# One attention block and a gated FFN on one core: batch 1's queries turned by DMA, batch 0 turned by products, gates begun in halves, and a new written order

## The chip, the core and the metric

The kernel runs on one core of one Trainium2 chip. The core has TensorE (PE, matrix products, with its weight loads shown as PEld), VectorE (DVE), ScalarE (ACT), GpSimd (POOL) and SyncE (SP), and 16 DMA engines. Each engine works through its own instructions in order; semaphores join them. PE writes into PSUM, which has eight banks of 128 x 512 f32. The metric is device time in microseconds, lower is better.

## The reference

Four batches of 768 tokens, eight heads of width 64. Each token attends to the 8 first keys (global) and to the 96 keys up to itself (local), with a bias that falls with distance; the result goes through a gated FFN.

```python
B, H, S, D = q.shape                                  # 4, 8, 768, 64
scores = scale * np.matmul(q, k.transpose(0, 1, 3, 2))
rel = pos[:, None] - pos[None, :]
is_global = pos[None, :] < 8
is_local = (rel >= 0) & (rel < 96)
dist = np.where(is_global & ~is_local, 96.0, np.abs(rel))
scores = scores - slopes[:, None, None] * dist        # then -1e9 where neither
a = softmax(scores); attn = np.matmul(a, v)
x = attn.transpose(0, 2, 1, 3).reshape(B * S, H * D)  # 3072 x 512
g = x @ w_gate                                        # 512 x 1536
out = (g * sigmoid(g) * (x @ w_val)) @ w_out          # 1536 x 512
```

## The kernel before

**Tiling.** The 3072 tokens are eight tiles of 384, two (halves) per batch. For a batch the eight heads form four pairs `hp`. Keys lie in 14 chunks of 64 rows: 8 global and 56 local ones; a chunk serves a window of 152 queries. Chunks are packed into units of two to four; batch 0 has other units (0 and 1 for its first half, 2 to 4 for its second), so that half 0 can go ahead.

**Attention steps.** Each step is a word in the string `ORDER`, followed by its numbers, and `@n` names a PSUM bank.

- `Lh`, `L4`, `Lr` load queries (i = 1) and keys (i = 0) of batch 0 by halves, of batch 1 four heads at a time, of batches 2 and 3 by single heads in 256-byte rows (L249, L287, L292). `Lv`, `Lt`, `LG` load V (L255, L261, L266), `Lw` a quarter-height piece of a gate or value weight (L299), `Lo` a third of `wo` (L307). All of these are issued by POOL and turn f32 into f16 on the way.
- `VG` loads the 8 global V rows of batch 0 (L271) and `Gc` copies them into the 14 chunks (L277); later batches do this by `G`, a DMA of SP (L283).
- `T` and `U` turn queries and keys of batches 0 and 1 on PE with an identity matrix, 8 and 16 turns a step (L358, L399); `k`, `q`, `kw`, `qw` copy the turned data out of PSUM (L367, L372, L390, L412). For batches 2 and 3 `D` turns by a DMA of SP (L420), and `K` spreads the keys into chunks (L427 to L430).
- `c` makes scores (L448), `x` exponentials on ACT (L457), `m` multiplies by a mask on DVE (L478). `w.b.h.0` sums the rows (L505), `w.b.h.1` and `.2` weigh V (L511), `i` and `r` invert and spread the sums (L521 to L529), `p` scales into `xT` on DVE (L540), one of two sides a step: blocks 0 and 2, or 1 and 3.

**FFN steps.** `g.t.f` and `v.t.f` make 128 gate or value columns of tile t, four products of 384 columns each (L553); `t` is a tanh on ACT (L559), `s` and `h` make the hidden block on DVE (L563, L570). `o.t.i.part` adds a quarter of the output of 128 tokens (L588; L585 for the last 128 tokens, in two halves of 256 columns), and `e` evicts it on ACT and stores it through SP (L602, L603; L597 to L600 for the last). `fill` are products of ones whose result nobody reads (L338).

**What sets the order.** The string alone: every engine gets its instructions in the order in which the steps stand. POOL's loads take turns on eight semaphores, so a load is not issued before the eighth one ahead of it has landed. The pool `st` has 7 buffers for loaded queries and keys, `qT` 6, `kN` (keys turned by DMA) 3, `at` 14. SP carries, in one queue, the first small loads, `G`, `D` and the output stores; a `D` that waits holds the stores behind it, and the other way round.

Of the kernel before, what the change touches and what calls it, by code (L numbers as in the profile page):

```python
# [16 lines left out]
CH = 64  # L17
# [41 lines left out]
m.0.0.4.V m.0.1.2.V t.0.4 s.0.7 g.0.0@2 t.0.5 Lw.1.1.1 m.0.0.2.V Lw.1.1.0 m.0.1.3.V m.0.1.4.V  # L59
v.0.4@4 Lv.0.0.7.13 t.0.0 s.0.5 s.0.4 m.0.0.3.V h.0.4 Lt.0.0 t.0.3 v.0.7@5 Lw.1.0.1 Lw.1.0.0 v.0.6@3  # L60
v.0.5@6 h.0.7 g.0.2@1 w.0.1.0@4 Lv.0.5.7.13 Lv.0.2.7.13 Lv.0.7.7.13 t.0.6 s.0.6 s.0.0 Lv.0.4.7.13
Lv.0.3.7.13 h.0.5 v.0.2@5 v.0.3@0 v.0.1@2 s.0.3 i.0.1 h.0.6 t.0.2 r.0.1 s.0.2 Lv.0.1.7.13 L4.1.1
Gc.1.1.A w.0.1.2@6 p.0.1.1 w.0.1.1@3 LG.1.0 g.0.1@1 v.0.0@6 p.0.1.0 h.0.2 Lw.0.2.1 g.1.1@7 L4.0.0
L4.0.1 v.1.6@3 Lw.1.2.0 h.0.3 t.0.1 s.0.1 g.1.4@5 h.0.0 v.1.3@0 g.1.3@1 t.1.1 t.1.4 s.1.1 s.1.4
v.1.4@4 t.1.3 g.1.6@7 s.1.3 Lw.0.2.0 g.1.0@5 Lw.1.2.1 h.0.1 t.1.0 s.1.0 v.1.0@6 h.1.0 h.1.4 Lo.1
t.1.6 v.1.1@1 Lo.0 Lv.1.4.0.13 h.1.1 U.3.0@2 kw.3.A Lo.2 U.1.1@5 U.2.1@6 U.1.0@4 U.0.0@1 s.1.6
qw.2.A h.1.3 g.1.2@2 g.0.9@7 U.2.0@6 kw.1.A Lr.2.1.3 g.1.7@0 g.0.8@4 t.1.2 s.1.2 kw.0.V h.1.6
v.1.2@2 qw.1.A t.0.9 Lr.2.1.2 Lr.3.1.1 Lv.2.3.0.13 t.1.7 s.0.9 v.0.8@3 v.1.7@5 s.1.7 Lv.1.2.0.13
Lv.1.1.0.13 h.1.2 Lt.1.1 LG.3.1 LG.1.1 v.0.9@1 g.0.10@7 Lv.1.6.0.13 t.0.8 v.0.10@0 s.0.8 h.1.7
kw.2.A Lr.3.0.6 t.0.10 c.1.0.0@4 h.0.8 c.1.0.2@2 U.3.1@6 s.0.10 v.0.11@7 x.1.0.2 m.1.0.2.V x.1.0.0  # L70
o.0.0.0@2 g.0.11@3 t.0.11 qw.3.V h.0.9 o.0.1.0@4 o.0.1.1 c.1.1.1@5 h.0.10 s.0.11 c.1.0.1@0 x.1.0.1
Lr.2.0.0 o.0.1.2 h.0.11 o.0.1.3 e.0.1 o.0.0.1 o.0.0.2 o.0.0.3 e.0.0 x.1.1.1 o.0.2.0@3 G.1.0 g.1.11@0
g.1.5@1 t.1.11 t.1.5 Lv.3.7.0.13 Lr.2.0.2 Lt.1.0 G.1.1 s.1.5 Lt.2.0 Lv.2.5.0.13 o.0.2.1 Lv.1.3.0.13
Lr.2.1.7 Lv.1.0.0.13 c.1.1.2@4 c.1.1.0@6 o.0.2.2 o.0.2.3 s.1.11 x.1.1.0 v.1.11@1 m.1.1.1.V g.1.10@0
Lv.3.6.0.13 g.1.8@6 h.1.11 m.1.0.0.V x.1.1.2 v.1.5@7 e.0.2 v.1.10@2 v.1.9@1 v.1.8@4 m.1.1.0.V
m.1.1.2.V t.1.10 Lv.1.5.0.13 t.1.8 s.1.8 h.1.5 c.1.0.3@5 m.1.0.1.V h.1.8 w.1.0.0@3 x.1.0.3 o.1.0.0@7
# [24 lines left out]
Lt.3.1 Lr.3.0.3 s.4.1 g.4.7@3 t.4.8 g.4.5@5 t.4.5 m.2.1.4.V s.4.8 g.4.4@6 v.4.8@1 g.4.11@7 h.4.1
# [31 lines left out]
def kernel(  # L133
# [525 lines left out]
```

## Time and profile before

| | |
|---|---|
| median of the runs shown | 245.4 us (245.36, 245.4, 252.1) |
| the profiled execution, in all | 247.71 us |
| its span, first to last instruction | 245.6 us |
| PE busy | 234.9 us, 96% of the span |
| DVE, ACT, POOL busy | 162.3, 105.4, 87.0 us |
| gate and value products (L553), wg and wv | 72.6 and 72.2 us, 384 each |
| output products (L588) | 64.6 us, 276 |
| turns on PE, batch 0 (L358), batch 1 (L399) | 6.1 and 3.7 us, 128 each |
| loads by POOL's queue | 14.20 MB written, 64656 packets |
| mean granted PE clock | 0.979 of full |

Busy times are those of single instructions merged, so an engine is busy where anything of its runs. Matmuls overlap, so their mean lengths add up to more than their share of time; what one costs in a row of many is read from the chain, where the steps of one engine follow one another. In the groups, the last column is the idle time of the engine just before them, with what ended it. In the slices of the span each digit is the busy share of a fortieth, 6.1 us.

### The profile page before, as it was taken

How to read it: one execution, taken by the hardware profiler on the slowest of the kernel's cores; microseconds unless marked ns; L12 is line 12 of the kernel's file. 1: busy time of each engine (PE TensorE's matmuls, PEld its weight loads, DVE VectorE, ACT ScalarE, POOL GpSimd, SP SyncE). 2: the span in 40 equal slices, each digit the busy share in tenths (PEclk: the TensorE clock that was granted, in tenths of full speed). 3: DMA queues.
4: the chain of work that ended last, by engine and by line, in shares of the span. 5: the costliest groups of instructions: out<-in, count | busy, mean ns of one | idle time of the engine just before them, and what ended most of it. 6: DMA issues, size and time to landing. Idle time of an engine off the chain costs nothing.

```text
span 245.6 us, 7237 instructions
## 1 busy us (share of the span) xinstructions
PE 234.9 (96%) x3112; PEld 137.3 (56%) x3112; DVE 162.3 (66%) x359; ACT 105.4 (43%) x191; POOL 87.0 (35%) x117
## 2 busy tenths in 40 slices
PE   8599999999999999999699999999999999999994
PEld 5376566664554555555355466545555655556643
DVE  5398998785275577837577769834898478505840
ACT  5495733745632533225573253235761142323321
POOL 8698695545999976980000000000000000000000
PEclk9858999999999999999999999999999999999999
DMA  7999999999999999999900374012000300021012
GB/s 103 161 160 161 179 141 178 206 195 91 173 173 144 180 137 160 120 159 200 115 3 0 120 168 42 0 45 88 3 0 15 121 0 3 0 85 43 3 42 86
DMA packets 82095, 24.57 MB, mean 100 GB/s; under 512 B 68896, under 2 KB 79120, under 8 KB 82064
## 3 DMA queue, kind: packets, MB, share of 16 engines
q0 software_dynamic: 64656, 14.20, 65.2%
q1 hardware_dynamic: 17224, 9.77, 18.5%
q8 instruction: 24, 0.39, 0.6%
q10 hardware_dynamic: 184, 0.14, 0.2%
q14 instruction: 7, 0.06, 0.1%
HBM read 28.51 MB, written 6.29 MB: 142 GB/s over the span
## 4 chain that ended last, share of the span: by engine, by line
PE 82%; DMA 9%; DVE 3%; POOL 2%; issue 1%; ACT 1%; ACTq 0%; POOLq 0%
PE PS L553 47%; PE PS L588 25%; PE PS L511 3%; DMA kN<-st 3%; DMA st<-in_q_dram 3%; DMA wv<-in_moe_w_val_dram 3%; PE PS L448 3%; PE PS L505 2%; PE PS L399 1%; PE PS L585 1%; POOL st L249 1%; DVE vS L277 1%; DVE qT L390 1%; ACT th L559 1%; DVE at L478 0%
## 5 line engine op out<-in xcount | busy, mean ns | idle before, releaser
L563 DVE SCALAR_TENSOR_TENSOR sl<-th,PS 128x384 f32<-128x384 f32 x96 | 50.8, 549 | 41.0 <-ACT th L559 40.4
L553 PE MATMUL PS<-xT,wg 128*128 128x384 f16 x384 | 72.6, 326 | 2.2 <-DVE hT L570 2.1
L553 PE MATMUL PS<-xT,wv 128*128 128x384 f16 x384 | 72.2, 326 | 0.1
L559 ACT ACTIVATE th<-PS 128x384 f32<-128x384 f32 x96 | 44.3, 491 | 59.0 <-PE PS L553 50.0
L588 PE MATMUL PS<-wo,hT 128*128 128x512 f16 x276 | 64.6, 379 | 0.0
L570 DVE TENSOR_TENSOR hT<-PS,sl 128x384 f16<-128x384 f32 x96 | 50.9, 552 | 10.4 <-PE PS L553 8.8
L553 PEld LDWEIGHTS <-wg 128*128 128x128 f16 x384 | 36.9, 98 | 28.2 <-issue 2.8
L553 PEld LDWEIGHTS <-wv 128*128 128x128 f16 x384 | 36.7, 98 | 25.6 <-DMA wv<-in_moe_w_val_dram 0.5
L588 PEld LDWEIGHTS <-hT 128*128 128x128 f16 x276 | 26.0, 98 | 28.7
L457 ACT ACTIVATE at<-PS 128x912 f16<-128x912 f32 (+1 forms) x40 | 31.6, 830 | 22.7 <-PE PS L448 22.6
L255 POOL DMA_DIRECT2D vS<-in_v_dram x40 | 33.2, 845 | 8.4 <-DMA wo<-in_moe_w_out_dram 3.0
L602 ACT ACTIVATE osb<-PS 128x512 f32<-128x512 f32 x23 | 13.7, 597 | 41.2 <-PE PS L588 41.2
L478 DVE TENSOR_TENSOR at<-at,masks 128x912 f16<-128x912 f16 (+5 forms) x56 | 22.5, 442 | 1.9 <-ACT at L457 1.9
L540 DVE TENSOR_TENSOR xT<-PS,rb 128x768 f16<-128x768 f32 x16 | 14.6, 952 | 7.2 <-PE PS L511 6.7
L292 POOL DMA_DIRECT2D st<-in_q_dram x16 | 14.4, 915 | 3.1 <-PE PS L553 1.4
L292 POOL DMA_DIRECT2D st<-in_k_dram x16 | 14.2, 912 | 0.5 <-DMA vS<-in_v_dram 0.5
L448 PE MATMUL PS<-qT,kT 64*64 64x152 f16 (+4 forms) x464 | 13.5, 238 | 0.5 <-DVE xT L540 0.4
L448 PEld LDWEIGHTS <-kT 64*64 64x64 f16 x464 | 8.6, 113 | 7.9 <-issue 6.8
L511 PE MATMUL PS<-at,vS 64*32 64x152 f16 (+4 forms) x1024 | 10.5, 218 | 0.4 <-issue 0.4
L511 PEld LDWEIGHTS <-vS 64*32 64x32 f16 x1024 | 9.3, 90 | 2.6 <-issue 2.3
L338 PE MATMUL PS<-ones 128*128 128x256 f16 x44 | 9.1, 387 | 1.2 <-DVE wg L304 1.2
L358 PE MATMUL PS<-ident,st 96*64 96x96 f16 x128 | 6.1, 268 | 3.0 <-DMA st<-in_k_dram 2.6
(50 smaller groups left out, 115.1 us busy)
## 6 DMA issues: line engine op xcount, KB each, us to landing
out_dram<-osb SPq DMA_DIRECT2D x23, 256.0 KB, 3.7
vS<-in_v_dram POOLq DMA_DIRECT2D x24, 91.0 KB, 5.6
wg<-in_moe_w_gate_dram POOLq DMA_DIRECT2D x6, 256.0 KB, 5.7
wv<-in_moe_w_val_dram POOLq DMA_DIRECT2D x6, 256.0 KB, 7.2
wo<-in_moe_w_out_dram POOLq DMA_DIRECT2D x3, 512.0 KB, 14.8
st<-in_q_dram POOLq DMA_DIRECT2D x16, 96.0 KB, 7.2
st<-in_k_dram POOLq DMA_DIRECT2D x16, 96.0 KB, 5.2
st<-in_q_dram POOLq DMA_DIRECT2D x4, 192.0 KB, 7.5
```

Source lines behind the costliest of these rows:

```text
L255: nc.gpsimd.dma_start(out=v_of(b)[CH * c + NG:CH * c + CH, c0:c1, j, :], in_=v[b, h, KC * c0:KC * c1, :].rearrange("(i p) d -> p i d", p=KC))
L292: nc.gpsimd.dma_start(out=stage(b, i, h % 2, True)[:, h // 4, :, h // 2 % 2, :], in_=KQ[i][b, h].rearrange("(t p) d -> p t d", p=128))
L448: nc.tensor.matmul(PS[64 * e:64 * e + 64, bank + hi, col:col + n], lhsT=kT_of(b, hp)[r, CH * c:CH * c + CH], rhs=qTs[b, hp][r, q0:q0 + n], ...
L457: nc.scalar.activation(out=at[:, :, 0:w], in_=PS[:, bank:bank + 2, 0:w], func=AF.Exp, scale=scale)
L478: ENG[e].tensor_mul(a2, a2, m2)
L511: nc.tensor.matmul(PS[r, bank + e, o:o + n], lhsT=V[s, c, j, what - 1::2], rhs=at[s, hi, col:col + n], start=first, stop=last, skip_group_ ...
L540: nc.vector.tensor_mul(x_of(2 * b + half)[:, side::2, :], PS[:, bank:bank + 2, 0:TB], rbs[b, half])
L553: nc.tensor.matmul(PS[:, bank, 0:TB], lhsT=w[:, c, 128 * f:128 * f + 128], rhs=xTs[t][:, c, :], start=(c == 0), stop=(c == NC - 1))
L559: nc.scalar.activation(out=th, in_=PS[:, gv[t, f, 0], 0:TB], func=AF.Tanh, scale=0.5)
L563: nc.vector.scalar_tensor_tensor(out=sl, in0=gv[t, f, "t"], scalar=1.0, in1=PS[:, gv[t, f, 0], 0:TB], op0=AluOp.add, op1=AluOp.mult)
L570: nc.vector.tensor_mul(hTs[t, f // 3][:, f % 3, :], PS[:, gv[t, f, 1], 0:TB], gv[t, f, "s"])
L588: nc.tensor.matmul(PS[:, bank, :], lhsT=lhsT, rhs=wo[:, f, :], start=(f == 0), stop=(f == NFF - 1))
```

## The change

- **Batch 1's queries by DMA.** The two four-head loads of queries become eight loads of single heads; four `tr_dma` steps of SP turn them, in place of four `U` steps and their copies `qw`. Batch 1's keys stay with `L4` and `U`.
- **Global V rows in fp16.** A step `Ga` copies the 8 rows of each side from f32 to f16 once (8 x 256); the four `Gc` copies then read f16. In the order all four stand ahead of batch 0's first keys; before, two stood later.
- **Batch 0 turned by products.** `T` issues an ordinary matmul with the identity as the moving operand, and its result in PSUM is f32 where it was f16.
- **First gates in halves.** The four blocks are added up in the order 0, 2, 1, 3, the order in which the two `p` steps give them. For f = 0 and 1 of the first tile the sum is split: `ga`, `va` add blocks 0 and 2, `gb`, `vb` blocks 1 and 3.
- **Last rows as 384 + 128 columns.** The last 128 tokens make 384 columns first, with their eviction on ACT, then all twelve products of the last 128 columns, evicted on DVE; both stores go through SP.
- **A new order** of all steps. The last `fill` behind the last output goes; 44 fill products stay, now all ahead of the first gate.
- Functions `ld_wide` and `widen_ident` are new, and no step of the order calls them.

The diff, cut; of the order only the part up to the first gates, the output of tile 0 and the end are shown:

```diff
-pre Y.0.1.0 Ld.S Y.0.0.0 Lh.1.0.0.2 Z.1 VG.S.0 Z.2 fill.4@0 fill.4@1 fill.4@2 fill.4@3 VG.A.1 Li.S
-fill.4@4 Lh.0.0.2.4 Z.0 M.0 fill.4@5 M.1 Gc.0.0.V Lh.0.0.0.2 T.1.0.1@6 q.1.0.V T.2.0.0@7 T.1.0.0@0
-Lh.1.1.2.4 M.3 T.0.0.0@1 T.0.0.1@2 Gc.0.1.A T.2.1.1@3 k.2.0.A k.1.0.V Lh.1.0.2.4 LG.2.1 Lh.1.1.0.2
-T.3.1.1@4 q.3.1.A q.0.0.V k.0.0.A T.3.0.1@5 q.3.0.V T.3.0.0@6 T.2.0.1@7 M.2 q.2.0.V T.1.1.1@0
-k.3.0.A T.0.1.1@4 q.2.1.V Lh.0.1.2.4 q.0.1.A c.0.1.1@1 c.0.0.0@5 Gc.1.0.V x.0.1.1 T.2.1.0@7 x.0.0.0
-k.2.1.V Lv.0.1.0.7 Lv.0.5.0.7 q.1.1.V Lh.0.1.0.2 T.3.1.0@3 k.3.1.A c.0.0.1@1 Lw.0.1.0 x.0.0.1
-m.0.1.1.V c.0.1.0@4 m.0.0.0.V x.0.1.0 T.1.1.0@6 T.0.1.0@7 Lv.0.2.0.7 k.0.1.V k.1.1.V c.0.1.2@0
-x.0.1.2 L4.1.0 Lv.0.0.0.7 fill.4@3 fill.4@2 Lv.0.7.0.7 Lv.0.3.0.7 m.0.1.0.V fill.4@5 m.0.0.1.V
-w.0.0.0@7 i.0.0 c.0.0.2@0 Lv.0.4.0.7 x.0.0.2 fill.4@6 c.0.0.3@2 x.0.0.3 Lv.0.6.0.7 Lw.0.1.1
-Lv.0.6.7.13 w.0.0.2@4 r.0.0 Lw.0.0.0 c.0.1.4@0 w.0.0.1@6 p.0.0.1 c.0.0.4@2 x.0.0.4 x.0.1.4 c.0.1.3@4
-p.0.0.0 U.0.1@2 qw.0.A Lw.0.0.1 g.0.7@3 t.0.7 x.0.1.3 g.0.6@0 Lt.0.1 g.0.4@1 g.0.5@6 g.0.3@7
...
+pre VG.S.1 Li.S VG.S.0 Z.1 Z.2 Lh.0.1.2.4 fill.2@3 fill.2@3 fill.2@0 Ld.A fill.2@1 Z.0 Ga.0.A Ga.1.V
+M.1 M.3 fill.2@7 fill.4@2 Lh.1.0.0.2 Lh.0.0.0.2 Gc.0.1.V Lh.1.0.2.4 Lh.0.0.2.4 Lh.1.1.0.2 fill.4@3
+M.0 Gc.1.1.A Gc.1.0.V T.1.0.1@4 Lh.0.1.0.2 fill.2@5 fill.4@2 Lv.0.5.0.7 Y.0.0.0 Gc.0.0.V fill.4@6
+Lv.0.7.0.7 Lv.0.3.0.7 Lv.0.0.0.7 T.2.1.0@0 T.1.0.0@1 q.1.0.A Lh.1.1.2.4 T.0.0.1@7 T.0.0.0@5 k.1.0.V
+k.0.0.A q.0.0.A T.3.0.1@4 T.2.0.1@3 Lv.0.4.0.7 Lw.1.0.0 q.3.0.V Lv.0.6.0.7 Lv.0.2.0.7 T.2.0.0@5
+T.3.0.0@1 k.3.0.A c.0.0.1@6 fill.4@2 T.1.1.1@4 q.2.0.V c.0.0.0@1 fill.4@3 Lv.0.1.0.7 x.0.0.1 k.2.0.V
+M.2 m.0.0.1.V c.0.1.1@5 k.2.1.V fill.4@3 x.0.0.0 q.1.1.V m.0.0.0.V x.0.1.1 T.1.1.0@7 T.3.1.0@3
+k.3.1.A Lw.0.0.1 Lw.0.0.0 Lv.0.7.7.13 c.0.1.0@0 T.0.1.1@2 q.0.1.A T.0.1.0@4 m.0.1.1.V k.1.1.A
+T.3.1.1@5 T.2.1.1@6 fill.2@3 x.0.1.0 Lw.1.0.1 fill.2@2 Lw.0.1.1 Lv.0.0.7.13 k.0.1.V q.2.1.A
+c.0.0.4@3 c.0.0.3@0 m.0.1.0.V x.0.0.4 w.0.0.0@7 x.0.0.3 q.3.1.V Y.0.1.0 c.0.1.3@4 w.0.0.1@2
+m.0.0.4.V i.0.0 r.0.0 Lt.0.1 c.0.1.4@0 Lw.0.1.0 Lv.0.3.7.13 x.0.1.3 w.0.0.2@6 Lv.0.1.7.13 L4.0.1
+m.0.0.3.V p.0.0.0 c.0.0.2@4 x.0.1.4 Lt.0.0 Lv.0.5.7.13 Lv.0.2.7.13 c.0.1.2@2 p.0.0.1 Lv.0.4.7.13
+Lw.1.1.1 ga.0.0@0 x.0.1.2 Lv.0.6.7.13 ga.0.1@1 gb.0.1 va.0.1@7 m.0.1.4.V t.0.1 va.0.0@6 Lw.1.1.0
...
+c.1.1.0@0 o.0.2.0@7 o.0.1.1 h.0.8 h.1.3 c.1.1.1@5 x.1.1.0 D.1.0.1 x.1.1.1 c.1.1.2@0 x.1.1.2 t.1.8
+m.1.1.2.V s.1.8 o.0.1.2 m.1.1.1.V o.0.1.3 e.0.1 o.0.2.1 o.0.2.2 o.0.2.3 o.1.2.0@3 Lv.1.7.0.13
...
+o.7.1.2 o.7.1.3 e.7.1 o.7.2.0@1 o.7.2.1 o.7.2.2 o.7.2.3 e.7.2 o.7.2.4@2 e.7.3

+    def narrow_first_globals(c, e):
+        r = slice(CH * c, CH * c + NG)
+        copy_on(e)(out=first16[r, :], in_=first[r, :])
...
-            in_=first[r, :].unsqueeze(1).broadcast_to([NG, 7, 4 * D]))
+            in_=first16[r, :].unsqueeze(1).broadcast_to([NG, 7, 4 * D]))
...
-                nc.tensor.transpose(
-                    t16[64 * hi:64 * hi + 64, PT * j:PT * j + PT],
-                    stage(0, i, half)[:, head(hp, hi), D * j:D * j + D], ident)
+                nc.tensor.matmul(
+                    PS[64 * hi:64 * hi + 64, bank, PT * j:PT * j + PT],
+                    lhsT=stage(0, i, half)[:, head(hp, hi), D * j:D * j + D], rhs=ident,
+                    start=True, stop=True, skip_group_check=True)
...
+    SIDES = (0, 2, 1, 3)
+    def products(bank, t, f, which, blocks):
...
-        for c in range(c0, c1):
+        for c in blocks:
...
-                rhs=xTs[t][:, c, :], start=(c == 0), stop=(c == NC - 1))
+                rhs=xTs[t][:, c, :], start=(c == SIDES[0]), stop=(c == SIDES[-1]))
...
+    LC = 384
...
+        c = slice(0, DM) if not last_rows(t, i) else slice(LC, DM) if part == 4 else slice(0, LC)
+        for f in range(NFF) if part == 4 else range(3 * part, 3 * part + 3):
...
+        if i == 3:
+            bank = at_bank["o", t, 2, 1]
+            oB = sb2.tile([128, DM - LC], FP32, name="osb", tag="th", bufs=3)
+            nc.vector.tensor_scalar_mul(oB, PS[:, bank, 0:DM - LC], 0.5)
+            nc.sync.dma_start(out=out[r0:r0 + 128, LC:], in_=oB)
+            return
...
+        "ga": lambda bk, t, f: products(bk, t, f, 0, SIDES[:2]),
+        "gb": lambda t, f: products(None, t, f, 0, SIDES[2:]),
```

More of the change, by code (lines that the diff above doesn't have):

```diff
@@ L59 @@
[L59 to L64, printed above, removed]
@@ L215 @@
     wo = sb.tile([128, NFF, DM], FP16, name="wo")
+    ident32 = sb.tile([PT, PT], FP32, name="ident32")
+    wide = {}
     first = sb.tile([128, 4 * D], FP32, name="first")
+    first16 = sb.tile([128, 4 * D], FP16, name="first16")
     KQ = (k, q)
@@ L251, in ld_half, with ld_wide, widen_ident @@
             in_=KQ[i][0, h, TB * half:TB * half + TB, :].rearrange("h (p j) d -> p h (j d)", p=PT))
+    def ld_wide(e, i, p, hi):
+        g = p // 2
+        if (i, g) not in wide:
+            wide[i, g] = sb.tile([PT, 2, JH, 2, D], FP32, name=f"wide{i}{g}")
+        QUE[e].dma_start(
+            out=wide[i, g][:, p % 2, :, hi, :],
+            in_=KQ[i][0, head(p, hi), 0:TB, :].rearrange("(p j) d -> p j d", p=PT))
+    def widen_ident():
+        nc.vector.tensor_copy(out=ident32, in_=ident)
     def ld_v(b, h, c0, c1):
@@ L378, in keys_half @@
         k3 = chunked(0, hp)
-        t3 = turned(at_bank["T", hp, half, 0], JH)
+        t3 = turned(at_bank["T", hp, half, 0], JH, True)
         if half == 0:
@@ L545 @@
     hTs, gv = {}, {}
-    def products(bank, t, f, which, c0, c1):
-        if c0 == 0:
+    SIDES = (0, 2, 1, 3)
+    def products(bank, t, f, which, blocks):
+        if blocks[0] == SIDES[0]:
             gv[t, f, which] = bank
@@ L591, in put_out @@
[L591 to L603 removed]
+        if part in (0, 4):
+            at_bank["o", t, i, part // 4], = bank
```

189 lines of the change are left out of this document (92 added, 97 removed).

## The prediction

> **What bounds the kernel now.** First the shares of the span and the slices of the page, to see which engine is never free, and when:
>
> ```profile
> PE 234.9 (96%) x3112; PEld 137.3 (56%) x3112; DVE 162.3 (66%) x359; ACT 105.4 (43%) x191; POOL 87.0 (35%) x117
> PE   8599999999999999999699999999999999999994
> PEclk9858999999999999999999999999999999999999
> DMA  7999999999999999999900374012000300021012
> PE 82%; DMA 9%; DVE 3%; POOL 2%; issue 1%; ACT 1%; ACTq 0%; POOLq 0%
> ```
>
> TensorE (PE) is busy in every slice but the first three and the last, the DMA engines through the first half. A busy PE is not a useful one, so next come stretches, from the view that gives each engine's busy time by stretch, and two merged lines of PE's timeline:
>
> ```profile
> 12.00:18.00 6.00, 5.84 (x135) 4.56 (x137) 5.28 (x12) 5.46 (x14) 6.00 (x9) 0.50 1.24 157
> 10.20:25.50 15.30, 14.31 (x404) 10.74 (x399) 13.40 (x34) 9.72 (x19) 13.84 (x20) 0.67 1.41 159
> 25.60:60.00 34.40, 34.27 (x506) 20.87 (x506) 28.37 (x63) 18.48 (x33) 20.52 (x29) 1.00 1.37 171
> 111.00:124.00 13.00, 10.85 (x113) 6.07 (x111) 8.38 (x21) 7.10 (x14) 0.00 (x0) 1.00 1.16 147
> 124.00:241.80 117.80, 117.80 (x1414) 67.09 (x1413) 77.47 (x159) 44.56 (x82) 0.00 (x0) 1.00 0.15 43
> ...
> 25.57 4.06 PE L553 MATMUL PS<-xT,wg 128*128 128x384 f16 x24
> 120.34 2.11 PE L553 MATMUL PS<-xT,wg 128*128 128x384 f16 x12 [2.06 <-DVE hT L570]
> ```
>
> Columns: stretch, length, then PE, weight loads, DVE, ACT, POOL busy, granted clock, DMA share, GB/s. Three parts show. Up to 25.57 us, where the first gate product starts, DVE is the busy engine (13.40 of 15.30 us) and the clock is partly halved. From 25.6 to 124 PE loses 0.13 us before 60 and 2.15 between 111 and 124. After 124 it never stops. So the time is the moment of the first gate, plus PE's own work, plus PE's waits, plus a tail after 241.8. A shorter order can save only in these four.
>
> **The change, part by part.** The unit costs of PE's work come from the chain of work that ended last (start, length, what, count):
>
> ```profile
> 33.18 0.57 PE PS L505 x36
> 35.81 1.32 PE PS L511 x134
> 45.13 1.99 PE PS L399 x80
> 54.29 0.52 PE PS L448 x24
> 59.14 3.99 PE PS L588 x18
> 111.41 8.12 DMA kN<-st
> 196.26 15.06 PE PS L553 x92
> ```
>
> *Batch 1's queries by DMA.* Four of eight `tr_whole` calls go, 16 turns each: 64 turns at 1.99/80 = 0.025 us take 1.6 us off PE, in a stretch where PE never idles, so all of it counts: **-1.6**. The evictions of these turns leave ACT and DVE too; neither is on the path there, so I count nothing. What comes instead is transfer work, priced below.
>
> *The key wait.* The 2.06 us of idle PE at 118 to 120 hang on DVE, which stood in `spread_keys` behind a key transpose that SP issued at 111.41 and that took 8.12 us; `tr_dma` for pair 2 of batch 2 stood in SP's queue behind the output rows of tile 2. In the new order SP issues the key transposes of pairs 0, 1 and 2 of batch 2 ahead of those outputs, and only pair 3 has to wait for a buffer. Their last row is POOL's 92nd load of 119 instead of the 95th of 113. The wait goes, **-2.1**; late next is pair 1 (a rival below).
>
> *The first gate.* These rows are DVE's and PE's timeline:
>
> ```profile
> 9.82 0.70 PE L358 MATMUL PS<-ident,st 96*64 96x96 f16 x24 [2.56 <-DMA st<-in_k_dram]
> 14.50 1.99 DVE L277 CAST vS<-first 8x1792 f16<-8x1792 f32 x1
> 16.42 0.66 DVE L367 COPY kT<-PS 128x8 f16<-128x8 f16 x3
> 18.48 2.60 PE L338 MATMUL PS<-ones 128*128 128x256 f16 x12
> 23.69 1.82 DVE L540 TENSOR_TENSOR xT<-PS,rb 128x768 f16<-128x768 f32 x2
> ...
> L390 DVE COPY qT<-PS 128x384 f16<-128x384 f16 x6 | 3.2, 547 | 2.0 <-PE PS L358 2.0
> ...
> L563 DVE SCALAR_TENSOR_TENSOR sl<-th,PS 128x384 f32<-128x384 f32 x96 | 50.8, 549 | 41.0 <-ACT th L559 40.4
> ...
> L478 DVE TENSOR_TENSOR at<-at,masks 128x912 f16<-128x912 f16 x2 | 1.2, 612 | 0.0
> L478 DVE TENSOR_TENSOR at<-at,masks 128x96 f16<-128x96 f16 x3 | 0.6, 194 | 0.0
> ```
>
> The keys that release DVE's run land at 9.8 in both orders (third load in each). From there to the end of `scaled` at 23.69 + 1.82 = 25.51 DVE runs nearly without a gap. The new order takes out of this run two query evictions (2 x 0.55), the 1.99 us copy of the global V rows, one set of half-1 key copies (0.66) and, as the gates begin with blocks 0 and 2, the second `scaled` (0.91): 4.66 us. It puts in a set of key copies that ACT made before (0.66), a query eviction (0.55), and the masks of two more units (0.61 and 2 x 0.19): 2.2 us. That gives 23.0 for the first `scaled`. But ACT gets the moved copies on top of its 9.72 us, in line with the exponentials that the masks wait for. So the ends are 23.0 and 25.5; I take the middle, 24.2. The first two half gates last 4 x 0.164 = 0.65 us and the second `scaled` 0.91, so PE waits 0.26 before the second halves. The gain is 25.57 - 24.2 - 0.26: **-1.1** (from -2.3 to +0.2).
>
> No row shows the fp16 copy of the global rows. All four copies now stand ahead of the first keys, where DVE waits anyway, so even at 1.99 us each they cost nothing; if the rows landed late, at most one copy (2.0) would fall on the run. *Turning by products* writes f32 where the transpose wrote f16, with the same operands. DVE's copy of 384 out of PSUM took 547 ns from f16 against 549 in the gates (L563) from f32, so I price it at zero on both sides; its effect on the clock is a rival.
>
> *Transfers.* Loads from POOL:
>
> ```profile
> 72.00:84.00 12.00, 12.00 (x203) 6.27 (x192) 5.69 (x10) 4.12 (x7) 12.00 (x15) 1.00 1.91 156
> 42.85 0.78 POOL L307 DMA_DIRECT2D wo<-in_moe_w_out_dram  x1 [1.03 <-DMA st<-in_k_dram]
> wo<-in_moe_w_out_dram POOLq DMA_DIRECT2D x1, 512.0 KB, 14.9
> ...
> st<-in_q_dram POOLq DMA_DIRECT2D x16, 96.0 KB, 7.2
> st<-in_q_dram POOLq DMA_DIRECT2D x2, 384.0 KB, 5.5
> kN<-st SPq DMA_TRANSPOSE x8, 9.2
> qT<-st SPq DMA_TRANSPOSE x8, 3.5
> ```
>
> Two loads of 384 KB become eight of 96 KB, all ahead of the last third of `wo`; three of the four new transposes run there too. At POOL's pace of 15 loads in 12 us the eight take 6.4 us; the two moved 768 KB, at 171 GB/s 4.6 us. A transpose moves 192 KB: between nothing, if it fills gaps, and 1.15 us at that rate; I take 0.4. Sum 6.4 - 4.6 + 3 x 0.4 = 3.0 us more before the last `wo` load has landed: 42.85 + 14.9 = 57.7 becomes 60.7. PE asks for it at `o.0.1.2`. From the first gate up to there the new order has 172 gate and value matmuls (172 x 0.164 = 28.2), 9 of the output (9 x 0.222 = 2.0), 64 turns (1.6), 36 scores (0.8) and one half's weighing (1.9): 34.5 us, so it asks at 24.2 + 0.26 + 34.5 = 58.9. It waits **+1.8**, between 0 and 4.0 (transposes at 1.15 each). Before, the same step started at 59.14, 1.4 after its weights. Batch 2's and 3's loads have slack after that, since their consumers come at 90 and later.
>
> The Trainium skill, "DMA: Bandwidth & Descriptors", section "Specifications", speaks against this edit: pieces under 512 B are written by read-modify-write and miss the full rate. The rows agree in direction: 96 KB took 7.2 us to land where 384 KB took 5.5. If the eight loads ran at half of 171 GB/s, an estimate from that page's rule, they would take 9.0 us in place of 6.4, and the time would be 2.6 above my sum.
>
> *Last rows as 384 + 128.* The same columns on PE. DVE then evicts 128 columns after PE's end, not 256:
>
> ```profile
> 241.88 0.42 DVE L598 TENSOR_SCALAR osb<-PS 128x256 f32<-128x256 f32 x1 [5.74 <-PE PS L585]
> ```
>
> About a third of 0.42 goes, with a smaller last store: **-0.2** (0 to -0.4); the wider first part is evicted beside PE's last 12 matmuls.
>
> *The rest of the new order* holds the same work in PE's stream (63 changes between kinds of product against 66). Its unseen waits I bound by 0 and the 2.15 us that the old order lost between 111 and 124, and take 0, the row of 25.6 to 60.
>
> **Sum:** -1.6 - 2.1 - 1.1 + 1.8 - 0.2 = -3.2 on a span of 245.6, so 242.4; the profiled execution took 247.7 in all, 2.1 around its span, which makes 244.5. The runs shown have a median of 245.4, 2.3 below the profiled one; the same difference there gives 242.2.
>
> **The rivals.** *A: all in time.* The `wo` rows land before PE asks and the clock stays at full rate, so DVE's run ends at 23.0: -1.6 - 2.1 - 2.3 - 0.2 = -6.2, 239.2; with the first gate at 24.2 it is 240.4. I put it at 239.8. For it: transfers overlap on 16 engines. Against: the DMA row is at 9 all through this stretch. On the clock, 12.00:18.00 reads 0.50 though PE was busy 5.84 of 6 us, mostly turning. The Trainium skill, "TensorE: Matmul & The Clock Gate", "What's actually happening", has the clock throttled by default and released after some 3.4 us of activity. By that rule alone those 6 us should have released it, so the trace does not agree for transposes; whether products count no run here shows. By the rule the result is A's 239.2.
>
> *B: transfers on the path.* The transposes cost 1.15 each and batch 1's last queries land after 9.2 us like the keys, not 3.5: the wait is 4.0, 244.4.
>
> *C: slower.* The clock stays at half until the gates run. 16 fills stand between the first key turns and the row sums, at 2.60/12 = 0.217 us each 3.5 us, now ahead of scores in PE's line; and of the first gates (4.06 us for 24 at full clock) some 2 us are lost. That is +4.4 in place of -1.1; `wo` is then in time: -1.6 - 2.1 + 4.4 - 0.2 = +0.5, 245.9, and up to 248.0 with all 4.06 doubled. It decides where PE's gates run 3.9 us later than now.
>
> *D: the key wait stays.* Pair 1's keys of batch 2 pass SP behind a query transpose that waits for late rows. Then the -2.1 is not had: 244.3.
>
> **How the numbers follow.** Forecast 0.42 (242.2, its own range 240.6 to 243.8), A 0.24, B 0.13, C 0.11, D 0.10. Two per cent, about what a measurement of this kernel can tell from no change, is 240.5 and 250.3. Below 240.5 lie 0.8 of A and a tenth of the forecast: 0.24. Above 250.3 only the tail of C and B: 0.04. The range leaves out the lowest third of A and the upper half of C: 239.0 to 246.5.
>
> **What would show it.** The first gate between 23 and 25.5, its second halves 0.3 later; the output products' wait for `wo` near 59 to 61; no wait of a value or gate product on DVE near 95 to 108; 64 rows of L399's kind instead of 128; the clock in 12 to 18. Wrong would be: a first gate after 26, a new wait over 1 us elsewhere, above all at the scores of batch 1 near 64 or at the weighing near 75.

## The result and the profile after

| | before | after |
|---|---|---|
| median | 245.4 us (5 runs: 244.09 to 252.1) | 242.41 us (5 runs: 241.13 to 242.73) |
| the profiled execution, in all | 247.71 us | 241.13 us |
| its span | 245.6 us | 239.2 us |

The ratio after to before is 0.989, with a 95% interval of 0.984 to 0.994: faster by 1.1%, inside the two per cent. (The ratios here and below leave out executions over 1.5% above the fastest of their kernel; the medians are of all.) The median agrees with the forecast of 242.2 to 0.2 us. The profiled executions lie 6.6 us apart, though, twice as far as the medians. That is the first thing to explain, since the forecast was summed on a profiled execution.

From the page of after, the busy shares, the granted clock in slices of the span, and the DMA queue named instruction (packets, MB, share of 16 engines):

```profile
PE 230.2 (96%) x3048; PEld 133.2 (56%) x3048; DVE 163.4 (68%) x362; ACT 99.7 (42%) x186; POOL 92.2 (39%) x123
PEclk9999999999999999999999999999999999999999
...
q8 instruction: 24, 0.39, 0.7%
```

The same stretches of after as were shown of before (stretch, length, then PE, weight loads, DVE, ACT, POOL busy, granted clock, DMA share, GB/s):

```profile
12.00:18.00 6.00, 5.40 (x144) 3.70 (x136) 5.15 (x20) 5.97 (x15) 5.45 (x8) 1.00 1.54 138
10.20:25.50 15.30, 12.53 (x392) 8.60 (x387) 13.35 (x42) 11.91 (x25) 12.93 (x18) 1.00 1.43 159
25.60:60.00 34.40, 33.32 (x452) 19.98 (x450) 28.37 (x60) 11.89 (x25) 23.64 (x33) 1.00 1.50 173
111.00:124.00 13.00, 13.00 (x135) 7.55 (x136) 10.76 (x22) 7.81 (x13) 7.90 (x10) 1.00 1.73 151
```

The clock reads full in all four, and PE has no idle time between 111 and 124 (2.15 us before). But from 25.6 to 60, where it had lost 0.13 us, PE now loses 1.08. PE's timeline and the end of DVE's show where (the bracket is the idle time ahead, with what ended it):

```profile
21.20 0.18 PE L475 MATMUL PS<-qT,kT 64*64 64x40 f16 x1 [0.99 <-issue]
22.89 1.15 PE L582 MATMUL PS<-xT,wg 128*128 128x384 f16 x6
24.51 0.99 PE L582 MATMUL PS<-xT,wv 128*128 128x384 f16 x5 [0.31 <-DMA wv<-in_moe_w_val_dram]
35.43 2.77 PE L582 MATMUL PS<-xT,wv 128*128 128x384 f16 x16 [1.08 <-DMA wv<-in_moe_w_val_dram]
236.25 0.29 DVE L623 TENSOR_SCALAR osb<-PS 128x128 f32<-128x128 f32 x1 [6.12 <-PE PS L614]
```

The first gate comes at 22.89 us instead of 25.57. It is followed by two waits for value weights, 1.4 us together, which this profile of before did not have. The kernel ends 2.95 us after 236.25; before, 3.72 us lay between 241.88 and the end. The "issue" in the first line is a wait with no releaser in the profile. It turns out to matter in most of the experiments.

### The profile page after: what moved, and what is told of

It reads as the page before. It is cut to its first block, busy times and chain, and to the rows that moved or that the text cites. A ratio compares the mean times of both kernels' runs of the same rounds, so it can differ in the third digit from the quotient of the medians.

```text
span 239.2 us, 7117 instructions
## 1 busy us (share of the span) xinstructions
PE 230.2 (96%) x3048; PEld 133.2 (56%) x3048; DVE 163.4 (68%) x362; ACT 99.7 (42%) x186; POOL 92.2 (39%) x123
## 4 chain that ended last, share of the span: by engine, by line
PE 84%; DMA 8%; POOL 5%; issue 1%; DVE 0%; POOLq 0%
PE PS L582 50%; PE PS L614 27%; PE PS L475 3%; PE PS L538 3%; DMA wg<-in_moe_w_gate_dram 3%; DMA st<-in_q_dram 3%; POOL vS L271 3%; DMA wv<-in_moe_w_val_dram 2%; PE PS L532 1%; POOL st L253 1%; POOL wv L319 1%; POOL wg L319 1%; PE PS L426 0%; DVE osb L623 0%; POOLq L670 0%
## 5 line engine op out<-in xcount | busy, mean ns | idle before, releaser
L614 PE MATMUL PS<-wo,hT 128*128 128x512 f16 (+2 forms) x300 | 67.9, 371 | 0.0
L614 PEld LDWEIGHTS <-hT 128*128 128x128 f16 x300 | 28.0, 98 | 29.3
L629 ACT ACTIVATE osb<-PS 128x512 f32<-128x512 f32 (+1 forms) x24 | 14.2, 593 | 34.1 <-PE PS L614 31.6
L312 POOL DMA_DIRECT2D st<-in_q_dram x24 | 21.1, 885 | 1.5 <-DMA wv<-in_moe_w_val_dram 1.5
L567 DVE TENSOR_TENSOR xT<-PS,rb 128x768 f16<-128x768 f32 x16 | 14.9, 951 | 1.8 <-PE PS L538 1.2
L475 PE MATMUL PS<-qT,kT 64*64 64x152 f16 (+4 forms) x464 | 12.4, 225 | 1.8 <-issue 1.0
L475 PEld LDWEIGHTS <-kT 64*64 64x64 f16 x464 | 8.0, 106 | 7.8 <-issue 6.4
L538 PE MATMUL PS<-at,vS 64*32 64x152 f16 (+4 forms) x1024 | 10.5, 218 | 0.0
L556 DVE STREAM_TRANSPOSE rb<-dR 128x768 f32<-128x768 f32 x8 | 7.8, 976 | 0.2
```

The source lines that it names most:

```text
L312: nc.gpsimd.dma_start(out=stage(b, i, h % 2, True)[:, h // 4, :, h // 2 % 2, :], in_=KQ[i][b, h].rearrange("(t p) d -> p t d", p=128))
L475: nc.tensor.matmul(PS[64 * e:64 * e + 64, bank + hi, col:col + n], lhsT=kT_of(b, hp)[r, CH * c:CH * c + CH], rhs=qTs[b, hp][r, q0:q0 + n], ...
L538: nc.tensor.matmul(PS[r, bank + e, o:o + n], lhsT=V[s, c, j, what - 1::2], rhs=at[s, hi, col:col + n], start=first, stop=last, skip_group_ ...
L567: nc.vector.tensor_mul(x_of(2 * b + half)[:, side::2, :], PS[:, bank:bank + 2, 0:TB], rbs[b, half])
L614: nc.tensor.matmul(PS[:, bank, 0:c.stop - c.start], lhsT=hTs[t, f // 3][:, f % 3, 128 * i:128 * i + 128], rhs=wo[:, f, c], start=(f == 0), ...
```

## The experiments

**The same two kernels once more.** A second profile of each tells what belongs to the kernel and what to one execution.

> The kernel before once more, for a second profile. Theory (the wait of 2.06 us for the keys of batch 2 belongs to the execution that was profiled, since a later issue of those keys changed nothing in the time): PE's idle time between 111 and 124 is another one, 0 to 1.6 us, and the span is shorter than 245.6 by about as much. Rival (the wait is the order's own): 1.8 to 2.3 us again.

```profile
111.00:124.00 13.00, 13.00 (x148) 7.49 (x147) 10.33 (x24) 9.54 (x18) 0.00 (x0) 1.00 0.65 118
...
25.63 4.06 PE L553 MATMUL PS<-xT,wg 128*128 128x384 f16 x24
29.90 2.77 PE L553 MATMUL PS<-xT,wv 128*128 128x384 f16 x16 [0.20 <-DMA wv<-in_moe_w_val_dram]
104.72 0.61 PE L511 MATMUL PS<-at,vS 64*32 64x152 f16 x52 [0.76 <-issue]
239.87 0.42 DVE L598 TENSOR_SCALAR osb<-PS 128x256 f32<-128x256 f32 x1 [5.74 <-PE PS L585]
```

The key wait is not there. The span is 243.6 us, 2.0 shorter than in the first profile, and the median of 10 runs is 245.39. So the theory held: the 2.06 us belonged to one execution. A wait named "issue" of 0.76 us is there instead, at 104.

> The changed kernel itself once more, for a second profile and more times on the chip of the three runs beside it. Theory (what the first gate gains is given back at the loads of weights behind it): the first gate may lie anywhere from 22.9 to 24.5 us, PE's waits for weights between 24 and 60 are the longer the earlier it lies, and the time is 242 to 243 us either way. Rival (the first gate counts in full): a later first gate makes the span longer by as much.

```profile
20.94 0.18 PE L475 MATMUL PS<-qT,kT 64*64 64x40 f16 x1 [0.75 <-issue]
22.87 1.15 PE L582 MATMUL PS<-xT,wg 128*128 128x384 f16 x6
28.23 0.51 PE L532 MATMUL PS<-at,ones 128*32 128x152 f16 x23 [0.66 <-issue]
35.12 1.15 PE L582 MATMUL PS<-xT,wv 128*128 128x384 f16 x6 [0.50 <-DMA wv<-in_moe_w_val_dram]
45.52 0.66 PE L426 MATMUL PS<-ident,st 96*64 96x96 f16 x22 [0.48 <-DMA st<-in_k_dram]
236.51 0.29 DVE L623 TENSOR_SCALAR osb<-PS 128x128 f32<-128x128 f32 x1 [6.12 <-PE PS L614]
```

The median is 241.45 us against 245.31 beside it, ratio 0.987 (0.985 to 0.990); the span is 239.5. The first gate stayed at 22.87, so this run alone does not tell the two theories apart. It does give a difference of two profiles that each lie within 0.3 us of their median: 243.6 - 239.5 = 4.1 us.

**Was the key wait worth its 2.1 us?** In the order of before one step moves:

```diff
-... D.2.1.1 o.2.1.1 ...  v.3.3@3 D.2.2.0 t.3.3 ...
+... D.2.1.1 D.2.2.0 o.2.1.1 ...  v.3.3@3 t.3.3 ...
```

> The kernel before, with one step moved: the second-half key transpose of pair 2 of batch 2 is issued ahead of tile 2's output stores instead of behind them. Theory (the key wait on SP's queue costs 2.1 us): PE's idle time between 111 and 124 falls from 2.15 us to under 0.3, and the time falls by 1.7 to 2.3 us. Rival (pair 2's keys come late for another reason, a buffer or their own rows): PE still waits 1 us or more there and the time falls by less than 1 us.

Median 245.74 us against 245.73, ratio 1.002 (0.999 to 1.006): the theory fell. The key wait is gone from its profile, but another transposed load is late in the same place, and this execution, too, lies above its median (247.21):

```profile
122.24 0.46 PE L368 MATMUL PS<-qT,kT 64*64 64x96 f16 x19 [1.59 <-DMA qT<-st]
```

**Products or transposes, and the clock.** First after with transposes again, then before with products (the reverse edit, with the copies reading f32):

```diff
-                nc.tensor.matmul(PS[64 * hi:64 * hi + 64, bank, PT * j:PT * j + PT], lhsT=stage(0, i, half)[...], rhs=ident, ...)
+                nc.tensor.transpose(t16[64 * hi:64 * hi + 64, PT * j:PT * j + PT], stage(0, i, half)[...], ident)
```

> The changed kernel, with batch 0's 128 turns made by transposes into f16 again; all else, the order too, stays. Theory (products keep the clock): the granted clock between 12 and 18 falls from 1.00 towards 0.50, the first gate product starts 1.5 to 3 us later than 22.89, and the time rises by 1 to 3 us. Rival (the fills between the turns keep the clock, whatever the turns are): the clock stays at 1.00, the first gate within 0.5 us of 22.89, the time within 0.5 us of the changed kernel's 242.4.

> The kernel before, with batch 0's turns made by products into f32; nothing else is changed. Theory: the clock between 12 and 18 rises from 0.50 to 1.00, the first gate comes 0.5 to 2 us earlier than 25.57, and the time falls by 0.5 to 2 us. Rival (the clock hangs on the order and its fills): the clock stays at 0.50 to 0.7 there, the first gate within 0.5 us, the time within 0.5 us of before.

With transposes after takes 242.43 us, ratio to before 0.984 (0.980 to 0.988), which cannot be told from after itself (0.987, 0.985 to 0.990). The first gate of its profile came at 24.47, 1.6 us later, as the theory had it; but after with the old last rows, which keeps the products, has it later still, at 25.22 (both rows below). With products before takes 246.14, ratio 0.998 (0.994 to 1.001). Before with products, in its own windows:

```profile
12.00:18.00 6.00, 5.82 (x140) 4.70 (x142) 5.42 (x13) 5.45 (x14) 5.90 (x8) 0.50 1.30 161
111.00:124.00 13.00, 13.00 (x149) 7.47 (x148) 9.96 (x24) 9.40 (x15) 0.00 (x0) 1.00 0.85 123
```

The clock is at half as before, so turning by products does not keep it. The mean clocks of all executions, as far as their records go, agree: 0.970 to 0.979 here, 0.966 to 0.979 in before beside it, and 0.985 to 1.00 in after with transposes, as in after. The second line is a third execution of before's order of steps, again without the key wait.

**The fills.** From after, every fill behind the first turn is taken out (26 products); into before go five groups of four.

```diff
-T.1.0.1@4 Lh.0.1.0.2 fill.2@5 fill.4@2 Lv.0.5.0.7 ... c.0.0.1@6 fill.4@2 T.1.1.1@4 ...
+T.1.0.1@4 Lh.0.1.0.2 Lv.0.5.0.7 ... c.0.0.1@6 T.1.1.1@4 ...
```

> The changed kernel without the fill products that stand behind the first turn of batch 0; their results are read by nobody. Theory (the fills between the turns bring the clock back within 3 to 4 us): the clock is at 0.50 for about 10 us from 10 to 12 us on, as in the kernel before. If the first gate hangs on DVE, it comes 0 to 1 us later and the time stays within 0.5 us; if it hangs on PE's clock, 1.5 us or more later. Rival (the clock hangs on the turns being products): it stays at 1.00, with an earlier first gate by up to 1 us.

The median is 246.1 us, ratio to before 1.002 (0.998 to 1.005): without these fills the change gains nothing. From the profiled execution, which took 248.78, 2.7 us above the median, so that its waits may be longer than a usual execution's:

```profile
27.00:30.00 3.00, 3.00 (x18) 1.38 (x11) 2.10 (x8) 1.67 (x3) 2.70 (x5) 1.00 1.56 181
...
11.81 0.85 PE L301 MATMUL PS<-ident,st 96*64 96x96 f16 x16 [0.27 <-DVE kT L318]
25.67 0.58 PE L457 MATMUL PS<-at,vS 64*32 64x152 f16 x31 [2.64 <-issue]
27.12 2.10 PE L501 MATMUL PS<-xT,wg 128*128 128x384 f16 x6
82.57 0.20 PE L457 MATMUL PS<-at,vS 64*32 64x48 f16 x3 [0.97 <-issue]
203.94 0.21 PE L457 MATMUL PS<-at,vS 64*32 64x40 f16 x8 [1.33 <-issue]
```

The first gate comes at 27.12, and its six products take 2.10 us where after's took 1.15: half speed, while the granted clock reads 1.00 for the same stretch. The clock column missed it: this trace holds no clock record before 30.4 us, and the column gives 1.00 where it has none. The Trainium skill, "TensorE: Matmul & The Clock Gate", section "Seeing it yourself", warns that the clock events in a profile can be unreliable; here they are missing. The expectation of a half clock after 10 us held by the durations (16 turns take 0.85 us at 11.81, where after's take 0.53 at 11.31). It held in other executions too: seven of the twelve have a mean clock of 0.958 to 0.972, where after's eleven have 0.985 to 1.00. But the larger part of this execution's loss is the idle time named "issue": 5.6 us in four places against 1.4 in after's second profile, of 7.4 us in all. Whether the fills earn their place by the clock or by what they do to this wait, the run does not separate.

```diff
-... T.3.1.1@4 ... T.2.0.1@7 ... c.0.1.1@1 ... T.3.1.0@3 ... T.1.1.0@6
+... fill.4@4 T.3.1.1@4 ... fill.4@7 T.2.0.1@7 ... fill.4@1 c.0.1.1@1 ... fill.4@3 T.3.1.0@3 ... fill.4@6 T.1.1.0@6
```

> The kernel before with five groups of four fill products put among the turns and scores of batch 0, each into the bank that the next step overwrites. Theory (the fills keep the clock): the half clock, which lasts 10 us before, lasts under 5 us; as DVE sets the first gate there, that comes 0 to 1 us earlier and the time moves by less than 1 us. Rival (the half clock costs PE its full loss on the path): the first gate comes 2 us or more earlier and the time falls by as much. Second rival (the fills stand in the way): the first gate comes later by up to 4.3 us, 20 times 0.217.

```profile
27.16 1.30 PE L473 MATMUL PS<-xT,wg 128*128 128x384 f16 x7
31.36 5.60 PE L473 MATMUL PS<-xT,wg 128*128 128x384 f16 x17 [2.90 <-issue]
```

Median 250.12 us, ratio 1.020 (1.016 to 1.025); the profiled execution took 252.39. The half clock lasts 6.8 us from 10.0 on, shorter than before's 10.2, but the first gate comes 1.6 us later, and a new wait of 2.90 us falls into the gates, after which 17 of them take 5.60 us, at half clock. The second rival is nearest, with more on top.

**What "issue" is.** In the order of PE's instructions (a weight load and a product count as two), the 2.64 us in after without fills stand at instruction 704, the 2.90 us in before with fills at 960, the 0.99 of after at 704, and the 0.66 of after's second profile at 960. The later two without fills stand at 2240 and 5568. All are 192 above a multiple of 256, to within the few records that a trace misses. The program has 24 such places, and the page counts 24 packets of 16 KB in the queue named instruction (0.39 MB for PE's 6096 weight loads and products). In windows of 0.25 us, each of these waits ends 2.4 to 3.5 us after the window in which such a packet moves: packet 17.75 and end 21.20 (after), 18.50 and 20.94 (after again), 23.00 and 25.67 (without fills), 28.75 and 31.36 (before with fills).

The traces of all 14 profiles, read packet by packet, leave little room for another cause: PE stands at such a place 23 times, and each time goes on 1.2 to 1.9 us after its block's packet ended; at the 298 places without a wait it never arrives earlier than 1.1 us after the packet. So PE waits there for its own instructions.

The price hangs on how fast it uses them up: after goes from instruction 448 to 704 in 3.8 us (16.40 to 20.20), and 109 products of the weighing run in 1.09 us without fills at 80.51. The packet also moves later while the loads run: in after 1.6 to 4.1 us behind PE's passing of the place before, up to 60 us, and at most 1.4 behind it after 125. The Trainium skill, "Runtime: NRT & Kernel Launch", section "Instruction fetch mechanics", has the blocks of 256 instructions and a queue of their own, and calls the cost mostly hidden. The blocks agree; the cost does not: up to 3.22 us in one place here.

In after itself the 0.99 and 0.75 us at 704 are hidden: DVE, on which the first gate hangs, runs on without a gap meanwhile, and PE still waits 0.24 and 0.48 us for its scaling step afterwards. Without the fills DVE's second scaling step waits 2.23 us for PE.

**Does an earlier first gate pay?** Two more DVE copies ahead of the first scaling step of after:

```diff
-m.0.0.3.V p.0.0.0 c.0.0.2@4
+m.0.0.3.V N.0 N.1 p.0.0.0 c.0.0.2@4
+    def delay_dve(c):
+        nc.vector.tensor_copy(out=scratch[r, :, :], in_=first16[r, :].unsqueeze(1).broadcast_to([NG, 7, 4 * D]))
```

> The changed kernel with two more copies on DVE, into a tile that nobody reads, right ahead of the first scaling step of half 0: about 1.06 us each, 2.1 us together. Theory (weights that land later bound the first gates): the first gate comes 2 us later than without, PE's waits for weights between 24 and 60 fall to under 0.3 us, and the time rises by 0.5 to 1.0 us only. Rival (the first gate counts in full): the time rises by 1.8 to 2.2 us.

```profile
24.41 0.18 PE L402 MATMUL PS<-qT,kT 64*64 64x40 f16 x1 [2.09 <-issue]
27.40 2.10 PE L509 MATMUL PS<-xT,wg 128*128 128x384 f16 x6
...
39.39 1.80 PE L509 MATMUL PS<-xT,wv 128*128 128x384 f16 x10
```

Median 245.16 us, ratio 0.999 (0.995 to 1.002): 3.7 us more than after beside it, outside both expectations. The copies took 2.15 us, but the gate came 4.5 us later, with a late start and the fetch wait in the same stretch, and then ran at half speed (2.10 for six). The value step that waits at 35.1 in after starts at 39.39, 4.3 later, without a wait. As a test of 2 us it failed; in this execution the delay ahead of the gates also cost clock.

The profiles of two other kernels serve better, as their first gate happened to be later at full speed: after with transposes, and after with the old last rows (below). Rows of the first, then of the second:

```profile
24.47 1.15 PE L582 MATMUL PS<-xT,wg 128*128 128x384 f16 x6
36.12 1.15 PE L582 MATMUL PS<-xT,wv 128*128 128x384 f16 x6
```

```profile
25.22 1.15 PE L582 MATMUL PS<-xT,wg 128*128 128x384 f16 x6
36.01 1.31 PE L582 MATMUL PS<-xT,wv 128*128 128x384 f16 x7
```

A gate later by 1.6 and by 2.35 us than in after's second profile moves the value step from 35.12 to 36.12 and 36.01, and neither waits for its weights there. The spans are 239.9 and 240.4 (0.6 of the latter in the tail) against 239.5. So, in these single executions, of the last 2.4 us at the first gate about 0.9 arrive 13 us later; the rest is taken by the weights that land then and by the fetch.

**Can the weights come earlier?** One load of batch 1's keys goes behind the value weights, and the key turns with it:

```diff
-... L4.0.1 m.0.0.3.V ... Lw.1.1.0 vb.0.1 ...
+... m.0.0.3.V ... Lw.1.1.0 L4.0.1 vb.0.1 ...
```

> The changed kernel, with the load of four heads of batch 1's keys moved behind the second row of value weights and the key turns that need it moved behind it too, so that each value weight row is issued one load earlier. Theory (PE's wait of 1.1 us for a value weight near 34.3 hangs on POOL's order of loads): that wait falls under 0.4 us and the time falls by 0.5 to 1.1 us. Rival (the DMA engines are full there, and something else lands late instead): the sum of PE's waits between 24 and 60 stays at 1.0 us or more and the time is within 0.3 us of the changed kernel's.

```profile
39.48 0.82 PE L501 MATMUL PS<-xT,wg 128*128 128x384 f16 x4 [1.23 <-DMA wg<-in_moe_w_gate_dram]
42.02 1.46 PE L501 MATMUL PS<-xT,wg 128*128 128x384 f16 x8 [0.51 <-DVE kT L318]
```

Median 244.15 us, ratio 0.993 (0.989 to 0.996), while after with transposes, in the same set, has 0.984. The wait for value weights went, and gate weights and keys were late instead, as the rival had it. The time was not the rival's: some 2 us slower than after with transposes, of which the two waits shown are 1.7. No version faster than after came out of this.

**The other parts.** Queries of batch 1 back on PE (two four-head loads, four `U`, four `qw`; `Lr` stands for all eight loads):

```diff
-Lr.1.1.7 ... Lr.1.1.0 D.1.3.1 D.1.2.1 D.1.1.1 D.1.0.1
+L4.1.1 L4.1.0 U.2.1@3 qw.2.A U.3.1@5 qw.3.A U.0.1@0 U.1.1@1 qw.0.A qw.1.V
```

> The changed kernel with batch 1's queries as before: two loads of four heads and 64 turns on PE with their four copies, in place of eight loads of single heads and four transposes of SP. Theory (the turns cost PE 0.025 us each where it never idles): 64 more rows of that kind, the same first gate, and the time rises by 1.4 to 1.8 us. Rival (the eight narrow loads cost as much as the turns did): the waits for weights and keys between 24 and 60 fall by 1 us or more and the time stays within 0.5 us.

```profile
23.66 0.18 PE L394 MATMUL PS<-qT,kT 64*64 64x40 f16 x1 [3.22 <-issue]
25.46 2.07 PE L501 MATMUL PS<-xT,wg 128*128 128x384 f16 x6
147.12 0.24 PE L457 MATMUL PS<-at,vS 64*32 64x96 f16 x11 [2.16 <-issue]
```

Median 251.15 us, ratio 1.024 (1.020 to 1.027), far outside both expectations. Against after's second profile the first gate is 2.6 us later, six gates lose 0.9 at half speed, PE waits 2.8 us in four places for copies and exponentials, a fetch wait of 2.16 stands at 145 where the 128 added instructions moved a block's edge deep into a weighing, another takes 0.41, and the turns are 1.6: 10.5 together, and 8.9 less the 1.6 us that after's second profile waits behind its first gate, against 9.8 measured (249.3 - 239.5). The price of the turns alone isn't separated by it.

The first gates whole again:

```diff
-ga.0.0@0 x.0.1.2 Lv.0.6.7.13 ga.0.1@1 gb.0.1 va.0.1@7 ... va.0.0@6 ... vb.0.1 ... vb.0.0 ... gb.0.0
+x.0.1.2 Lv.0.6.7.13 g.0.1@1 ... v.0.1@7 ... v.0.0@6 ... g.0.0@0
```

> The changed kernel with the first two gate and value steps of tile 0 whole, where it has them in halves. Theory (PE has nothing else to do while DVE makes the second scaling step of 0.9 us): PE's first gate product starts 0.3 to 0.9 us later than 22.9, and the time rises by 0.3 to 0.9 us. Rival (a value weight that lands later takes the gain): PE's waits for weights between 24 and 60 fall by as much as the gates come later, and the time stays within 0.3 us.

Median 243.54 us, ratio 0.988 (0.983 to 0.992), the same as after's 0.987. The interval is 2.2 us wide, so it rules out neither the theory's 0.3 to 0.9 us nor the rival. The profile cannot show the waits exchanged, since the fetch wait there was 2.04 us and the gate came at 26.87.

The last rows in two parts of 256 again, without the last fill:

```diff
-... o.7.2.3 e.7.2 o.7.2.4@2 e.7.3
+... o.7.2.3 e.7.2
```

> The changed kernel with the last 128 tokens in two parts of 256 columns as before, the first stored through ACT's queue; the last fill product stays away. Theory (the tail is the last eviction and its store): from the end of PE to the end of the span it takes 0.1 to 0.8 us more than the 2.95 us of the changed kernel, and the time rises by as much. Rival (the tail of before was longer for its last fill product): those 2.95 us stay within 0.1.

```profile
236.85 0.43 DVE L628 TENSOR_SCALAR osb<-PS 128x256 f32<-128x256 f32 x1 [6.12 <-PE PS L615]
```

The span ends at 240.4, 3.55 us after this start, against 2.95 of after: the theory held in the profile, with 0.6 us. The time did not follow: 242.24 us, ratio 0.984 (0.981 to 0.987). 0.6 us is below what these runs resolve.

## Why the prediction was right, and where it was not

**The total was right: 242.2 against 242.41.** Several of its terms were not, and that they cancelled to 0.2 us is luck. The two second profiles (243.6 and 239.5) give the account: first gate 25.63 to 22.87, -2.8; tail, from DVE's last eviction to the end, 3.7 to 3.0, -0.7; PE's waits between gate and tail, 0.20 + 0.76 in before against 0.66 + 0.50 + 0.48 in after, +0.7; and the rest of the time between gate and tail, PE's own work, 213.3 to 212.0, -1.3. That is the -4.1 measured. Of the prediction's signs, 64 rows of turns and no wait near 95 to 108 came. Its sign of being wrong, a new wait over 1 us elsewhere, came too, with 1.08 us at 35.43 in the first profile (0.50 in the second).

- *Turns, -1.6.* 64 rows of that kind are left of 128, as said. PE's own work fell by 1.3 us in the second profiles and by 1.9 in the first two, around the 1.6; no experiment shows it by itself.
- *Key wait, -2.1.* This step failed, and it was counted twice. The wait was absent in two further executions of before's order, and issuing those keys earlier moved nothing. It was what put the profiled execution 2.3 us above the median: the second profile, without it, lies 0.3 above (245.69 in all). The sum took 2.1 off and then carried the same 2.3 over to after. Counted once, its other terms add up to -1.1 and 244.3; the second profiles differ by 4.1, and the missing 3.0 is in the gate and PE's waits (2.8), the tail (0.5), less 0.3 of PE's own work. Without it after's profiled executions lie 1.3 below its median (first set) and 0.1 below (second). Rival D, the wait's return, had no object.
- *First gate, -1.1.* The middle of 23.0 and 25.5 was too late: 22.89 and 22.87. The DVE run of the lower bound was sized well: 12.7 us, from DVE's first key copy at 9.78 to the end of the first scaling step near 22.5 (half of the row below), against 12.8 (10.23 in before to 23.0). It began 0.45 earlier, and the gate came 0.4 behind it, after scores that stand ahead in PE's order; that 22.89 meets 23.0 is these two cancelling. DVE waited 1.5 us for ACT in this run, against 1.2 in before, so ACT's added copies cost little. The second half gates did not wait the 0.26 either.

```profile
21.55 1.81 DVE L567 TENSOR_TENSOR xT<-PS,rb 128x768 f16<-128x768 f32 x2
```

- *Wait for `wo`, +1.8.* It did not come: PE takes the output products at 59.5 without a wait. POOL issued the last `wo` load at 50.16, and the three landed after 9.1 to 10.7 us, not 14.9 (POOL's and PE's timeline, and the view of the tile `wo`):

```profile
50.16 0.75 POOL L327 DMA_DIRECT2D wo<-in_moe_w_out_dram  x1 [2.03 <-DMA wo<-in_moe_w_out_dram]
59.51 4.71 PE L614 MATMUL PS<-wo,hT 128*128 128x512 f16 x21
```

```profile
DMA to landing us min/median/max: 9.1/10.0/10.7
```

  So the load was issued 4.3 us later than the sum had it (42.85 + 3.0), landed 5.8 us faster, and was there at 59.3, 0.2 ahead of PE's step; the sum had 60.7 and 58.9. Here too two errors cancel. PE waits for value weights at 24.5 and 35.1 to 35.4 instead, 0.5 to 1.4 us. No run shows that the narrow loads cause these: POOL issued the weight awaited at 35.43 at 29.43, and its first narrow load at 31.82; whether the two share the engines to the weight's cost stays open. Gate and waits together were put at +0.7 and measured -2.1.
- *Tail, -0.2.* Mis-sized, -0.8 in the first profiles and -0.7 in the second: the old last rows account for 0.6 of it; the rest went with the fill or is not resolved.
- *Clock.* Left to a rival with the products as its cause. Products are not the cause, as before with products shows. In after's second profile 3.4 us are at half, from 7.55 on; its first has no clock record before 10.23, and eight turns took 0.53 us there at 6.17 against 0.36 in the second, so that part ran at half too. Among after's executions that much has no visible effect on the time: in the second set 241.39 and 241.55 us at a mean clock of 0.993, 241.37 to 241.47 at 0.999 and 1.00; one at 0.985 took 242.83. The rows below this point are the stretches of half clock in before, in before with fills, and in after with transposes. A clock between 0.5 and 1 tells how much of a stretch was at half: of 10 to 11 in before (1 - 0.78)/0.5 = 0.44 us. It lasts 0.44 + 9 + 0.8 = 10.2 us, 6.8 and 3.4 us (13.7 in before's second profile): with fills among the turns it is shorter, and each is a multiple of 3.4. What sets it off stays open. Ahead of it PE had stood for keys or queries (2.56 us in before, 2.01 in after's second profile), but in after with whole gates 1.54 us up to 6.27 were followed by 4.6 us at full clock. The Trainium skill, "TensorE: Matmul & The Clock Gate", "What's actually happening", has activity judged in free-running windows of 3.4 us. The lengths agree with that. The prediction read 5.84 busy us out of 6 against the rule; as the clock stayed at half, busy in that column was not the activity that frees it.

```profile
10.00:11.00 1.00, 0.66 (x28) 0.53 (x26) 0.77 (x4) 0.00 (x0) 0.71 (x1) 0.78 1.48 191
11.00:20.00 9.00, 8.71 (x168) 6.61 (x167) 7.78 (x23) 7.24 (x15) 7.75 (x11) 0.50 1.48 152
20.00:21.00 1.00, 1.00 (x6) 0.56 (x4) 1.00 (x4) 0.00 (x0) 1.00 (x2) 0.60 1.33 190
```

```profile
10.00:16.00 6.00, 5.99 (x90) 4.44 (x91) 2.87 (x9) 2.25 (x7) 5.12 (x7) 0.50 1.40 155
16.00:17.00 1.00, 1.00 (x26) 0.53 (x27) 1.00 (x2) 0.25 (x1) 1.00 (x3) 0.59 1.32 175
```

```profile
12.00:15.00 3.00, 3.00 (x52) 1.88 (x47) 2.12 (x8) 2.35 (x5) 2.41 (x4) 0.50 1.58 140
15.00:16.00 1.00, 1.00 (x22) 0.57 (x21) 0.01 (x1) 0.72 (x1) 1.00 (x2) 0.81 1.06 128
```

- *Rival A* gave 239.2 by a sum that had the key wait in it too; its -6.2 meets the 6.4 between the first two spans only because that execution of before was a long one. *B*'s wait for `wo` did not come. *C*, a first gate 3.9 us late, did not happen in after. After without its fills has *C*'s time, 246.1 us against 245.9, but not its mechanism: no fills stand in the way, and the gate is 1.6 us later than before's.

What the prediction had no term for is PE's fetch of instructions. In before's first profile it is one wait of 0.36 us at 104.18, named "issue", in the stretch from 60 to 111 that the prediction's list of PE's losses leaves out; the other steps of the page's 1% "issue" are not at a block's edge. Reading the order as free beside its products ("unseen waits 0") was right here by luck of where the blocks' edges fall: waits of 2 us or more stand at such edges in the profiles of five of the other orders.

Open stays why the packets of instructions are later in one execution than in another, and what part of the gain belongs to the halves and to the fp16 rows: whole gates moved nothing measurable, and the fp16 rows were not tried by themselves.

## What to carry to other kernels

A wait that one profile shows may belong to that execution: before it is counted as a gain, see a second profile, or ask whether it explains why the profiled time lies above the median, and then count it once. In a fully written-out stream PE can wait for its own instructions at every 256th of them, in these runs worst behind runs of very short products and while the loads fill the DMA engines, so adding or removing small products early can cost 2 to 3 us elsewhere. Products that nobody reads can be worth their place, but fills put among the turns of the other order made that kernel 2% slower.

## What the runs showed that was not expected

- PE's instruction blocks: 256 instructions, waits from 0.28 to 3.22 us, at 704 in every profile of after's orders and at 3008 in every one of before's (at 960 and 1472 with its fills), and once 1.33 us at 202, where POOL has no load left.
- The granted clock read 1.00 over products that ran at half speed (2.10 against 1.15 us for six), because the trace had no clock record there. The duration of a known product is the safer gauge.
- One copy of 8 x 1792 with a repeated source took 2.0 us on DVE from f32 and 1.06 from fp16, as three in a row in after show:

```profile
3.62 3.17 DVE L297 COPY vS<-first 8x1792 f16<-8x1792 f16 x3
```
